# Inverting the softmax sums from doubled rows in DRAM in a four-layer attention kernel

## The chip, the core and the metric

The kernel runs on one core of a Trainium2 chip. The metric is the device time of one execution in microseconds. Before the change it is 1423.88 us, the median of 3 runs (1420.51 to 1424.61).

The core has TensorE (PE in the profile; PEld is its weight load), VectorE (DVE), ScalarE (ACT), GpSimd (POOL) and SyncE (SP), each with an in-order queue of its own. Nearly all transfers are issued from SyncE's queue, a few small ones from ScalarE's; sixteen DMA engines carry them.

## The reference, cut to what matters

Four residual layers run over 2048 tokens of width 512 with 32 heads of 16: A, B, A, B. Layer A is a linear attention with learned feature maps; layer B splits the tokens into four segments of 512 and mixes, per head, causal softmax attention inside the segment with a memory of the earlier segments:

```python
def phi(t): return jnp.where(t > 0, t + 1.0, jnp.exp(t))
for s in range(4):                       # segments of 512 tokens
    qs, ks, vs = q[:, :, s], k[:, :, s], v[:, :, s]
    p = softmax(qs @ ks.T * scale + mask)
    a_dot = p @ vs
    a_mem = (phi(qs) @ M) / ((phi(qs) @ z)[..., None] + 1e-6)
    outs.append(g * a_mem + (1.0 - g) * a_dot)
    M, z = M + phi(ks).T @ vs, z + phi(ks).sum()
x = x + concat(outs) @ wo
```

Both `a_dot` and `a_mem` are a numerator over a sum for each token and head. These divisions are what the change is about.

## The kernel before

**Layout.** In layer B the data of a segment lie transposed: heads and their 16 features along the 128 partitions, the 512 tokens along the row. A chunk `c` (0 to 3) is one such tile and holds eight heads. A turn `m` (32 in a layer) is half a chunk: segment, chunk, half `hf` with four heads. `LayerB.steps` walks through five steps in each turn and places every other piece of work (projections, output products, loads) at a step written by hand; `at(k + j, f)` puts a function on step `k + j`, `due` calls it. The wrappers `Ordered` and `mm` tie every instruction to the one before it on its engine, so each queue runs in the order of the program text.

**A turn on the engines.** SyncE copies projected queries and keys into the operand tiles (`stack`, six transfers a chunk half; `e<-ta` in the profile). TensorE computes logits twice: once for the row maxima (`maxima`; the banks `mx` and `my`, reduced by VectorE), once for the weights (`attend`; bank `lg`, exponentials by ScalarE, the causal triangle cut by GpSimd's affine selects). The maxima are transposed, negated and written by a transfer from ScalarE's queue into a row of the query tile (`put_maxima`; `e<-mt`). TensorE multiplies the weights by the values (`weighted`; bank `pv`), ScalarE moves the result into tile `U`, which holds numerators and sums.

**The division.** A numerator tile has 128 partitions (eight heads of 16 features), but there are only eight rows of sums, one for each head. They go through DRAM:

- `gather` (L1136) writes the half's numerators to the tile `num` (`tmp<-U`) and its four rows of sums to the DRAM tile `den` (`den<-U`).
- For the memory part `read` (L1076) writes four rows of sums from each of two tiles (`den<-mmq`, `den<-ot`).
- `invert` (L1110) has four steps. `compact` loads the sums as a dense tile over 128 partitions: 64 columns wide (`dn`) where both parts are there, 32 (`dm`) where there is one. `flip` is a reciprocal on VectorE. `put` writes it back to DRAM (`inv<-dn`, `inv<-dm`). `load` reads, for each part, eight rows of 512, each repeated sixteen times, into a tile of 128 partitions (`KN<-inv` for the attention's part, `mmq<-inv` for the memory's).
- `close` (L1145) has GpSimd multiply numerators by inverted sums (`tmp<-tmp,KN` and `ot<-ot,mmq`) and add the parts; ScalarE and GpSimd split the sum into a high and a low part for the output product.

The steps come from the tables `GATHER`, `READ`, `INVERT` and `JOIN`; the two loads of one chunk are issued together, and often `stack`'s copies of the next chunk half stand right behind them. The two layers B have 32 inversions (20 with `dn`, 12 with `dm`) and 52 such loads of 256 KB each. In the last segment of a layer only some chunks go this way; the others are divided on VectorE after a transposition (`finish`).

Of the kernel before, what the change touches and what calls it, by code (L numbers as in the profile page):

```python
# [15 lines left out]
D = 512  # L16
H = 32
DH = 16
P = 128
# [106 lines left out]
def interleave_kernel(ctx, tc, x_in, a_wqkv, a_wphi, a_wo, b_wq, b_wk, b_wv, b_wo, b_beta,  # L126
# [15 lines left out]
    def nm(s):  # L142
        uid[0] += 1
        return f"{s}_{uid[0]}"

    def T2(tag, bufs, dt=F32, shape=(P, 512)):
        return sp.tile(list(shape), dt, tag=tag, bufs=bufs, name=nm(tag))

    def PS(tag, bufs, shape=(P, 512)):
        return ps.tile(list(shape), F32, tag=tag, bufs=bufs, name=nm(tag))  # L150
# [38 lines left out]
    dve, act, pool, sync = [Ordered(e) for e in (nc.vector, nc.scalar, nc.gpsimd, nc.sync)]  # L189
# [10 lines left out]
    def mm(*a, **k):  # L200
        n = a[0].free_size()
        work[0] += n / 2.26 if k["rhs"].dtype == F32R else (n * 2 / 2.4 + 25 if "tile_position" in k else 2 * max(112, n * 2 / 2.4))
        return held(nc.tensor.matmul(*a, **k))  # L203
# [55 lines left out]
    def dtile(shape, name):  # L259
        return dr.tile(list(shape), F32, name=name)  # L260
# [745 lines left out]
    class LayerB:  # L1006
# [69 lines left out]
        def read(self, s, c, k):  # L1076


            kn, ph = self.summed(s, c)[1], self.st[s, c]["phi", 0]
            pn = [PS("pv", PV), PS("g", G)]  # L1080
            for a in range(2):
                mm(pn[a][0:68, :], lhsT=kn[64 * a : 64 * a + 64, :], rhs=ph[64 * a : 64 * a + 64, :],
                   start=True, stop=True, tile_position=(64 * a, 0))
            old = self.old[s, c] = T2("ot", OT)
            upper = T2("mmq", 2)
            for t, p in zip((old, upper), pn):
                act.activation(t[0:68, :], p[0:68, :], AF.Identity, bias=bd[0:68, 26:27])

            def dens():
                d = self.den(s, c)  # L1090
                for a, t in enumerate((upper, old)):
                    sync.dma_start(out=d[12 - 4 * a : 16 - 4 * a], in_=t[64:68, :])

            def numerators():
                sync.dma_start(out=old[64:128, :], in_=upper[0:64, :])
            self.at(k + READ[0], dens)
            self.at(k + READ[1], numerators)
            if s == NSEG - 1 and c >= self.cut:
                self.invert(s, c, k + READ[2], range(1, 2), INVERT[2][c])

                def scaled():
                    pool.tensor_tensor(out=old, in0=old, in1=self.inv.pop((s, c, 1)), op=MUL)
                self.at(k + READ[3], scaled)

        def den(self, s, c):
            if (s, c) not in self.dens:
                self.dens[s, c] = dtile((16, D), nm("den"))
            return self.dens[s, c]

        def invert(self, s, c, k, parts, steps):  # L1110


            lo, hi = 8 * parts[0], 8 * parts[-1] + 8
            n = (hi - lo) * 4
            tiles = {}

            def compact():
                d = tiles["d"] = T2("dn" if n == 64 else "dm", 1, shape=(P, n))
                sync.dma_start(out=d[:, 0:n], in_=self.den(s, c)[lo:hi].rearrange("h (x i) -> (h x) i", i=n))

            def flip():
                dve.reciprocal(tiles["d"][:, 0:n], tiles["d"][:, 0:n])

            def put():
                tiles["i"] = dtile((hi - lo, D), nm("inv"))
                sync.dma_start(out=tiles["i"].rearrange("h (x i) -> (h x) i", i=n), in_=tiles["d"][:, 0:n])

            def load():
                for i in parts:
                    t = self.inv[s, c, i] = T2(*(("mmq", 2) if i else ("KN", 1)))  # L1130
                    rows = tiles["i"][8 * i - lo : 8 * i - lo + 8].unsqueeze(1).broadcast_to([8, DH, D])
                    sync.dma_start(out=t, in_=rows)
            for j, f in zip(steps, (compact, flip, put, load)):
                self.at(k + j, f)

        def gather(self, s, c, hf, U):  # L1136
            if hf == 0:
                self.num[s, c] = T2("tmp", 2)
            sync.dma_start(out=self.num[s, c][64 * hf : 64 * hf + 64, :], in_=U[1 - hf : P : 2])
            sync.dma_start(out=self.den(s, c)[4 * hf : 4 * hf + 4], in_=U[31 * hf : P : 32])  # L1140

        def outputs(self, s, c):
            return [T2("oh", OO, F32R), T2("ol", OO, F32R)]
# [518 lines left out]
```

## Time and profile before

| what | value |
|---|---|
| median of 3 runs | 1423.88 us |
| profiled execution | 1420.89 us, span 1419.2 us |
| granted TensorE clock | 0.999 |
| transfers of all DMA queues | 222.72 MB, 157 GB/s in the mean |
| loads of inverted sums | 28 to `KN`, 24 to `mmq` |
| writes of sums | 56 from `U`, 24 from `mmq`, 24 from `ot` |

The span runs from the first to the last instruction of one profiled execution; the 1.7 us beside it lie around it. Lines of a group give busy time, the mean of one instruction in ns, and the idle time of the engine just before with what ended it. Most engine instructions go through one helper and bear its line, L181; matmuls bear L203, transposes L207; so groups are told apart by the names of the tiles, written as result<-operands. In a timeline row the brackets give the engine's idle time ahead of the instruction and what ended it. A stretch of windows has its length, the engines' busy times, the granted clock, the mean share of the sixteen DMA engines and GB/s.

### The profile page before, as it was taken

To read this page: it belongs to the slowest core of one execution; us is meant where nothing else is said; L and a number is where in the kernel's file an instruction comes from. 1 tells how busy PE (TensorE), PEld (TensorE's weight loads), DVE (VectorE), ACT (ScalarE), POOL (GpSimd) and SP (SyncE) were. 2 spreads that over 40 slices of the span, in tenths; PEclk is the share of its full clock that TensorE was granted. 3 is DMA by queue.
4 is the path that set the end of the run, shared out by engine and by line. 5 is a ranking of instruction groups with operands and counts; after the bars stand their busy time and mean duration, and the time that the engine had idled before them with its cause. 6 is when DMAs were issued, how large, how long until landed. Compare 5 with 4: busy or idle time off the path is not lost.

```text
span 1419.2 us, 33171 instructions
## 1 busy us (share of the span) xinstructions
PE 1373.8 (97%) x12070; PEld 946.3 (67%) x12070; DVE 953.1 (67%) x3028; ACT 810.0 (57%) x1246; POOL 733.8 (52%) x1073
## 2 busy tenths in 40 slices
PE   9999999999999999999999999999999999999997
PEld 7787778765666565665568887886656565666554
DVE  5766888677666556577546768958776665666663
ACT  5555345447676576566544434553666765765654
POOL 1678765325566556554524446641446565654543
PEclk9999999999999999999999999999999999999999
DMA  5369285536655546466640104854465565555541
GB/s 196 119 220 335 92 267 187 173 115 186 186 132 167 167 133 179 147 162 196 173 146 31 61 31 132 266 177 144 129 185 147 148 182 158 146 165 145 142 143 68
DMA packets 134898, 222.72 MB, mean 157 GB/s; under 512 B 26032, under 2 KB 39472, under 8 KB 134736
## 3 DMA queue, kind: packets, MB, share of 16 engines
q1 hardware_dynamic: 132768, 219.96, 52.0%
q8 instruction: 97, 1.59, 0.5%
q10 hardware_dynamic: 1968, 0.64, 0.2%
q14 instruction: 65, 0.53, 0.1%
HBM read 115.54 MB, written 41.55 MB: 111 GB/s over the span
## 4 chain that ended last, share of the span: by engine, by line
PE 74%; DVE 7%; ACT 6%; DMA 5%; POOL 4%; issue 2%; SPq 1%; ACTq 0%; DVEq 0%; POOLq 0%
PE g L203 45%; PE pv L203 8%; PE lg L203 8%; PE mx L203 4%; PE g L207 3%; ACT P L181 3%; PE my L203 3%; POOL P L181 2%; PE lg L207 2%; DMA e<-ta 1%; SPq L181 1%; DVE es L181 1%; POOL tb L181 1%; POOL tmp L181 1%; DVE junk L181 1%
## 5 line engine op out<-in xcount | busy, mean ns | idle before, releaser
L181 ACT ACTIVATE P<-lg 128x1024 f32<-128x1024 f32 x316 | 324.8, 1028 | 172.5 <-PE lg L203 152.0
L181 POOL TENSOR_SCALAR_AFFINE_SELECT P<-P 128x256 f32<-128x256 f32 (+1 forms) x448 | 190.1, 439 | 399.0 <-ACT P L181 394.8
L181 DVE CUSTOM_DVE_ANT_0 junk<-mx,mask 128x128 uint8<-128x128 f32 (+2 forms) x384 | 147.2, 421 | 116.3 <-PE my L203 86.8
L203 PE MATMUL g<-hh,wqk 128*128 128x512 f32 x512 | 185.2, 410 | 0.7 <-ACT mt L181 0.7
L203 PE MATMUL lg<-e,e 64*128 64x512 f32 (+1 forms) x1010 | 166.3, 387 | 12.3 <-ACT P L181 10.8
L203 PE MATMUL g<-w,oh 128*128 128x512 f32 x508 | 169.5, 414 | 0.5 <-ACT hh L181 0.4
L203 PE MATMUL pv<-P,v 128*32 128x512 f32 (+3 forms) x2048 | 165.1, 439 | 4.4 <-ACT ot L181 4.3
L181 DVE CUSTOM_DVE_ANT_0 mx<-mx,mask 128x512 f32<-128x512 f32 x128 | 89.1, 696 | 114.6 <-PE my L203 93.6
L203 PEld LDWEIGHTS lg<-e,e 64*128 64x128 f32 x1010 | 80.1, 184 | 109.9 <-issue 50.7
L203 PE MATMUL my<-e,e 63*128 63x256 f32 (+3 forms) x519 | 148.1, 345 | 4.3 <-DVE mxs L181 3.2
L203 PE MATMUL mx<-e,e 63*128 63x256 f32 (+3 forms) x519 | 147.0, 336 | 2.2 <-DVE mxs L181 1.9
L181 DVE CUSTOM_DVE_ANT_0 junk<-my,mask 128x128 uint8<-128x128 f32 (+2 forms) x384 | 146.7, 420 | 0.0
L203 PE MATMUL g<-w,hh 128*128 128x512 f32 x448 | 144.0, 402 | 0.3 <-ACT hh L181 0.3
L203 PEld LDWEIGHTS pv<-P,v 128*32 128x32 f32 x2048 | 53.6, 109 | 106.4 <-issue 93.9
L203 PEld LDWEIGHTS g<-hh,wqk 128*128 128x128 f32 x512 | 96.2, 188 | 32.3 <-issue 11.8
L203 PEld LDWEIGHTS g<-w,oh 128*128 128x128 f32 x508 | 87.9, 189 | 30.3 <-issue 13.2
L203 PE MATMUL g<-w,ol 128*128 128x512 f32 x254 | 101.2, 398 | 2.9 <-DVE ol L181 2.1
L203 PE MATMUL g<-hl,wqk 128*128 128x512 f32 x256 | 100.3, 392 | 0.0
L181 DVE DVE_READ_ACCUMULATOR2_ANT mxs<- 128x1 f32 x1024 | 100.1, 98 | 0.0
L203 PEld LDWEIGHTS mx<-e,e 63*128 63x128 f32 (+1 forms) x519 | 90.5, 186 | 11.1 <-DVE mxs L181 4.8
L203 PEld LDWEIGHTS g<-w,hh 128*128 128x128 f32 x448 | 80.3, 188 | 22.9 <-issue 6.3
L203 PEld LDWEIGHTS my<-e,e 63*128 63x128 f32 (+1 forms) x519 | 83.9, 185 | 16.9 <-DVE mxs L181 8.7
(189 smaller groups left out, 2835.9 us busy)
## 6 DMA issues: line engine op xcount, KB each, us to landing
e<-ta SPq DMA_DIRECT2D x384, 128.0 KB
wqk<-wqk SPq DMA_DIRECT2D x64, 512.0 KB
x<-x SPq DMA_DIRECT2D x48, 256.0 KB
xr<-x SPq DMA_DIRECT2D x32, 256.0 KB
x<-xr SPq DMA_DIRECT2D x28, 256.0 KB
tmp<-U SPq DMA_DIRECT2D x56, 128.0 KB
KN<-inv SPq DMA_DIRECT2D x28, 256.0 KB
pq<-tb SPq DMA_DIRECT2D x24, 256.0 KB
```

Source lines behind the costliest of these rows:

```text
L181: i = f(*a, **k)
L203: return held(nc.tensor.matmul(*a, **k))
L207: return held(nc.tensor.transpose(*a))
```

## The change

Each row of sums is written to DRAM twice, by a transfer whose source repeats the row; the DRAM tile has 16 rows of 2 x 512. `compact` and `put` carry twice as much, so the dense tiles are 128 and 64 columns wide. The DRAM tile of inverted sums then has each row twice in a row, and `load` takes sixteen rows, each repeated eight times. The values that arrive in the 128 partitions are the same. No step of the tables is changed.

```diff
             def dens():
                 d = self.den(s, c)
                 for a, t in enumerate((upper, old)):
-                    sync.dma_start(out=d[12 - 4 * a : 16 - 4 * a], in_=t[64:68, :])
+                    sync.dma_start(out=d[12 - 4 * a : 16 - 4 * a], in_=t[64:68, :].unsqueeze(1).broadcast_to([4, 2, D]))
...
-                self.dens[s, c] = dtile((16, D), nm("den"))
+                self.dens[s, c] = dtile((16, 2, D), nm("den"))
...
             lo, hi = 8 * parts[0], 8 * parts[-1] + 8
-            n = (hi - lo) * 4
+            n = (hi - lo) * 8
...
             def compact():
-                d = tiles["d"] = T2("dn" if n == 64 else "dm", 1, shape=(P, n))
-                sync.dma_start(out=d[:, 0:n], in_=self.den(s, c)[lo:hi].rearrange("h (x i) -> (h x) i", i=n))
+                d = tiles["d"] = T2("dn" if n == P else "dm", 1, shape=(P, n))
+                sync.dma_start(out=d, in_=self.den(s, c)[lo:hi].rearrange("h u (x i) -> (h u x) i", i=n))

             def flip():
-                dve.reciprocal(tiles["d"][:, 0:n], tiles["d"][:, 0:n])
+                dve.reciprocal(tiles["d"], tiles["d"])

             def put():
-                tiles["i"] = dtile((hi - lo, D), nm("inv"))
-                sync.dma_start(out=tiles["i"].rearrange("h (x i) -> (h x) i", i=n), in_=tiles["d"][:, 0:n])
+                tiles["i"] = dtile((2 * (hi - lo), D), nm("inv"))
+                sync.dma_start(out=tiles["i"].rearrange("h (x i) -> (h x) i", i=n), in_=tiles["d"])

             def load():
                 for i in parts:
                     t = self.inv[s, c, i] = T2(*(("mmq", 2) if i else ("KN", 1)))
-                    rows = tiles["i"][8 * i - lo : 8 * i - lo + 8].unsqueeze(1).broadcast_to([8, DH, D])
+                    rows = tiles["i"][2 * (8 * i - lo) :][0:16].unsqueeze(1).broadcast_to([16, DH // 2, D])
                     sync.dma_start(out=t, in_=rows)
...
-            sync.dma_start(out=self.den(s, c)[4 * hf : 4 * hf + 4], in_=U[31 * hf : P : 32])
+            sync.dma_start(out=self.den(s, c)[4 * hf : 4 * hf + 4],
+                           in_=U[31 * hf : P : 32].unsqueeze(1).broadcast_to([4, 2, D]))
```

## The prediction

> **What bounds the kernel now.** I read the page's busy times, then the chain that ended last, then the chain in order of time, then TensorE's own idle times, and last the DMA around the loads that the change touches.
>
> ```profile
> span 1419.2 us, 33171 instructions
> PE 1373.8 (97%) x12070; PEld 946.3 (67%) x12070; DVE 953.1 (67%) x3028; ACT 810.0 (57%) x1246; POOL 733.8 (52%) x1073
> PE 74%; DVE 7%; ACT 6%; DMA 5%; POOL 4%; issue 2%; SPq 1%; ACTq 0%; DVEq 0%; POOLq 0%
> ```
>
> TensorE is busy 1373.8 of 1419.2 us, so about 45 us are all that any unhidden wait can give back. The chain puts 5% on DMA. What the change can win must be found where a late transfer holds TensorE up, and that is a few short places. First, how wide the loads of the inverted sums run (timeline of SyncE's queue, then windows; the last two columns are the mean busy share of the 16 DMA engines and GB/s):
>
> ```profile
> 695.48 0.60 SPq L181 DMA_DIRECT2D mmq<-inv  x1
> 702.60 2.82 SPq L181 DMA_DIRECT2D e<-awk  x6
> ...
> 697.50:698.50 1.00, 1.00 (x12) 0.61 (x5) 0.40 (x2) 0.29 (x1) 0.31 (x1) 1.00 0.50 177
> 703.50:705.50 2.00, 2.00 (x11) 1.35 (x10) 1.93 (x5) 1.02 (x3) 1.54 (x3) 1.00 0.86 223
> ```
>
> From 697.5 to 698.5 almost nothing but two of these loads is under way (`KN<-inv` was issued just ahead of `mmq<-inv`), and the share stands at 0.50; once plain weight loads have joined, at 703.5, it is 0.86. Loads of eight rows repeated sixteen times keep half of the engines busy and leave the other half idle. Their effect on what is queued behind them (chain in order of time: start, us, what):
>
> ```profile
> 529.47 7.05 DMA mmq<-inv
> 586.98 5.97 DMA e<-ta
> 653.10 2.49 DMA e<-ta
> 694.75 5.68 DMA KN<-inv
> 972.78 2.48 DMA ot<-x
> ```
>
> A plain 256 KB load took 2.48 us and a 128 KB copy of projected rows 2.49 us where the queue was free; the row loads, 256 KB too, took 5.68 and 7.05 us, and a copy issued right behind a pair of them 5.97 us.
>
> **The change part by part.** Gains first. TensorE's idle times that I trace back to such a landing (timelines of TensorE, then of ScalarE, VectorE and GpSimd):
>
> ```profile
> 483.27 0.56 PE L203 MATMUL lg<-e,e 64*128 64x256 f32 x4 [0.95 <-ACT P L181]
> 540.01 0.56 PE L203 MATMUL lg<-e,e 64*128 64x256 f32 x4 [0.43 <-ACT P L181]
> 681.18 1.28 PE L203 MATMUL pv<-P,v 128*32 128x512 f32 x16 [1.15 <-ACT ot L181]
> 683.15 0.50 PE L203 MATMUL lg<-e,e 64*128 64x512 f32 x2 [0.69 <-DMA mmq<-inv]
> 687.34 0.46 PE L203 MATMUL mx<-e,e 63*128 63x512 f32 x1 [0.50 <-DVE mxs L181]
> 702.21 0.56 PE L203 MATMUL lg<-e,e 64*128 64x256 f32 x4 [0.71 <-ACT P L181]
> 1179.19 0.56 PE L203 MATMUL lg<-e,e 64*128 64x256 f32 x4 [0.79 <-ACT P L181]
> 1370.80 1.28 PE L203 MATMUL pv<-P,v 128*32 128x512 f32 x16 [0.50 <-ACT ot L181]
> 1373.89 0.38 PE L203 MATMUL mx<-e,e 63*128 63x256 f32 x1 [1.10 <-DVE mxs L181]
> ...
> 538.37 0.52 ACTq L181 DMA_DIRECT2D e<-mt  x1
> 538.93 1.02 ACT L181 ACTIVATE P<-lg 128x1024 f32<-128x1024 f32 x1 [2.56 <-DMA mmq<-inv]
> 701.13 1.02 ACT L181 ACTIVATE P<-lg 128x1024 f32<-128x1024 f32 x1 [1.03 <-DMA KN<-inv]
> 1178.12 1.02 ACT L181 ACTIVATE P<-lg 128x1024 f32<-128x1024 f32 x1 [1.28 <-DMA e<-ta]
> 685.82 0.69 DVE L181 TENSOR_TENSOR xr<-g,xr 128x512 f32<-128x512 f32 x1 [4.35 <-DMA xr<-x]
> 674.59 1.30 POOL L181 TENSOR_TENSOR tmp<-tmp,KN 128x512 f32<-128x512 f32 x1 [6.66 <-DMA mmq<-inv]
> ```
>
> ScalarE's exponentials stand behind an issue of the maxima row (538.37), and that issue waits for an earlier transfer that is none of its data; so a late row load stops ScalarE, and TensorE misses the freed bank of the logits. How much sooner the loads land I take from the clean window: two loads, 512 KB, at half the engines. If the same bytes use all of them, their moving part halves. A lone row load has 2.48 us as its floor (the plain load), so a single one gains at most 5.68 - 2.48 = 3.2 us and a copy behind a pair at most 5.97 - 2.49 = 3.5 us; at the low end 0, since the bytes stay. In crowded stretches all engines are busy already:
>
> ```profile
> 588.00:592.00 4.00, 4.00 (x32) 2.48 (x31) 2.87 (x12) 2.05 (x2) 1.33 (x3) 1.00 0.94 233
> 670.00:675.00 5.00, 5.00 (x41) 3.02 (x40) 3.00 (x12) 2.63 (x3) 0.41 (x1) 1.00 0.76 200
> 1172.00:1176.00 4.00, 4.00 (x32) 2.55 (x24) 2.61 (x12) 1.62 (x2) 1.86 (x3) 1.00 0.99 246
> ```
>
> With a share of 0.94 to 0.99 spreading saves less there than at 0.76. I take 1.2 us sooner in crowded stretches, 2 us in the others.
>
> - 483.27 and 1179.19: ScalarE's wait of 1.28 us loses most of its length; of 0.95 + 0.79 = 1.74 us I take 1.5.
> - 540.01: the wait of 2.56 us shrinks below 1; with the small stops just behind it 0.6.
> - 681 to 703: GpSimd would start its product 2 us sooner (674.59), but selects that wait for exponentials stand between, so 0.7 of the 1.15 us; of 0.69 I take 0.3; the residual load (4.35 us of VectorE's waiting) comes 1 us sooner, 0.5; at 702.21 all 0.7. Sum 2.2.
> - 1370.80 to 1373.89: the first gap only, 0.5. The second is ended by VectorE behind a plain load, whose delay I cannot put on the row load before it.
> - Scattered waits of ScalarE behind copies, as at 586.98: 0.6.
>
> Gains: 1.5 + 0.6 + 2.2 + 0.5 + 0.6 = 5.4 us; bounds 0 and, all the rows listed with 0.6 of scattered ones, 0.95 + 0.43 + 1.15 + 0.69 + 0.50 + 0.71 + 0.79 + 0.50 + 1.10 + 0.6 = 7.4 us.
>
> Costs. The inversion works on twice the columns (groups by line; issues by tile, with least, median and longest ns; VectorE's timeline):
>
> ```profile
> L181 DVE RECIPROCAL dn<-dn 128x64 f32<-128x64 f32 x20 | 11.0, 548 | 0.4 <-DMA dn<-den 0.4
> L181 DVE RECIPROCAL dm<-dm 128x32 f32<-128x32 f32 x12 | 4.2, 348 | 2.2 <-DMA dm<-den 2.2
> ...
> L181 SPq DMA_DIRECT2D den<-U x56: 522/542/607, 324.0 to 1367.7; - x56
> L181 SPq DMA_DIRECT2D den<-mmq x24: 266/436/876, 385.2 to 1374.1; - x24
> L181 SPq DMA_DIRECT2D den<-ot x24: 271/288/623, 386.1 to 1374.5; - x24
> L181 SPq DMA_DIRECT2D KN<-inv x28: 628/657/670, 338.0 to 1384.6; - x28
> L181 SPq DMA_DIRECT2D xr<-x x32: 343/430/1171, 429.6 to 1374.8; - x32
> ...
> 526.65 0.55 DVE L181 RECIPROCAL dn<-dn 128x64 f32<-128x64 f32 x1
> 530.37 0.42 DVE L181 CUSTOM_DVE_ANT_0 junk<-mx,mask 128x256 uint8<-128x256 f32 x1 [1.52 <-PE my L203]
> ```
>
> 32 more columns cost 548 - 348 = 200 ns. So 20 inversions grow by 400 ns and 12 by 200: 8.0 + 2.4 = 10.4 us of VectorE. Behind the one at 526.65 stand four maxima, then VectorE idles 1.52 us for TensorE: 0.4 us fits into that. The idle time is the cover; without it all 10.4 us would show. I take the chain's 7% of VectorE, 0.7 us; bounds 0 and 10.4.
>
> The 104 writes of sums (56 + 24 + 24) carry 16 KB for 8 KB. Repeating rows makes an issue dearer by at most 657 - 430 = 227 ns, by these rows, and by nothing at least: 0 to 24 us of SyncE; I take 100 ns, 10 us. SyncE is 1% of the chain, hence 0.1 us. Behind a write SyncE waits for its landing before it may issue the compacting load, and behind that stand six copies; then it waits for the longer reciprocal before the write back. Only one of these waits is near TensorE, the late `dm` in the table (2.2 us in all): 0.2 us. The compacting loads and the write backs move 64 KB for 32 in runs twice as long, as many runs as before: nothing, covered by the steps between. Costs: 0.7 + 0.1 + 0.2 = 1.0 us.
>
> Net: 5.4 - 1.0 = 4.4 us less. The profiled execution took 1420.9 us (span 1419.2 and 1.7 around it), so 1416.5; it lies 3.0 us under the median of the runs, 1423.9, and against that the sum is 1419.5.
>
> [...]
>
> **The rivals.**
>
> *Hidden anyway.* TensorE sets the pace, other transfers fill the engines (0.94 to 0.99), and the steps of the schedule leave room. Each stop above also has a second cause: at 540 the same place in the second layer, without the wait of 2.56 us, still shows idle time (1243.05 below). Then gain and cost cancel: 1423.9 less 0 to 2, about 1423.
>
> ```profile
> 1243.05 0.49 PE L203 MATMUL lg<-e,e 64*128 64x512 f32 x2 [0.59 <-ACT P L181]
> ```
>
> *Slower through the inversion.* The longer reciprocal sits in VectorE's in-order queue ahead of the maxima whose banks TensorE waits for. It decides if the idle time behind an inversion is under the 0.4 us added. At 526.65 it is not. If 0.4 us shows at the 20 large ones and the gains do not come: 1423.9 + 8 = 1432; with half of the gains, 1429.
>
> *It does not spread.* The number of engines could follow something other than the sixteen rows, or eight engines could be a limit of reading one row many times. Then the costs alone are left: 1423.9 + 1 = 1425. The share of 0.86 with weight loads shows only that other shapes spread.
>
> **How the numbers follow.** Main forecast 0.58, hidden 0.15, slower through the inversion 0.20, no spread 0.07. A measurement of this kernel can tell about 0.3% from no change: 1419.6 and 1428.2 are the limits. Of the main case 0.40 lies under 1419.6 and 0.18 inside, gains of half the size (1423.9 - 2.7 + 1.0 = 1422.2) among them; of the hidden one 0.01 under, 0.12 inside, 0.02 above; the inversion gives 0.03 inside and 0.17 above; no spread 0.04 inside and 0.03 above. So faster 0.41, same 0.37, slower 0.22. The main case alone runs from 1423.9 - 7.4 = 1416.5, less 3 for the spread of the runs, 1413, to 1423. The range goes from there to 1429, the inversion with half of the gains.
>
> **What would show it.** Right: the share while only row loads run near 0.9 or more and not 0.5; chain entries of copies behind them of 3 to 5 us; no wait of 2.56 us at 538.9 and less at 483, 681 and 702; reciprocals of some 950 and 550 ns without a new idle time of TensorE behind them. Wrong: a share of still 0.50; or the share doubled and TensorE's idle time unchanged (hidden); or new waits of TensorE for maxima right behind reciprocals, or for copies behind a SyncE that waits for the sums. A time above 1428 or below 1413 would mean that I have missed a mechanism.

## The result and the profile after

| | before | after |
|---|---|---|
| median | 1421.12 us (16 runs, 1416.73 to 1424.61) | 1417.42 us (16 runs, 1415.16 to 1419.61) |
| ratio to before, 95% interval | | 0.9977 [0.9966, 0.9987] |
| profiled execution | 1420.89 us, span 1419.2 us | 1417.35 us, span 1415.6 us |

The change makes the kernel faster by 0.23%: 3.7 us between the medians, 3.6 us between the two profiled spans. The forecast was 4.4 us. The median of before fell from 1423.88 us to 1421.12 us as more runs came in, so of the two forms of the forecast only the difference is to be compared. The sixteen runs of before spread over 7.9 us, twice the effect: a single stop in a single profiled execution proves little, and the experiments below are read by their ratios first.

The page of the changed kernel, its span, busy times and shares of the chain that ended last:

```profile
span 1415.6 us, 33171 instructions
PE 1371.6 (97%) x12070; PEld 944.6 (67%) x12070; DVE 961.9 (68%) x3028; ACT 810.2 (57%) x1246; POOL 734.0 (52%) x1073
PE 73%; DVE 8%; ACT 6%; POOL 5%; DMA 3%; issue 3%; SPq 1%; ACTq 0%; DVEq 0%; POOLq 0%
```

DMA's share of the chain goes from 5% to 3%, VectorE's from 7% to 8%. That is the direction which the prediction had laid out, but it shows little: e2 and e6 below, with the short reciprocals of before, have VectorE at 9%. TensorE's own busy time falls by 2.2 us though it runs the same 12070 matmuls; that is read at the end of the layer, below. Two stretches of the changed kernel (length, five engines, granted clock, DMA share, GB/s):

```profile
697.50:698.50 1.00, 1.00 (x12) 0.57 (x5) 0.45 (x2) 0.25 (x1) 0.36 (x1) 1.00 0.90 246
670.00:675.00 5.00, 5.00 (x41) 3.17 (x39) 1.99 (x7) 1.59 (x2) 0.19 (x1) 1.00 1.03 273
```

Where the share stood at 0.50 with two row loads alone under way it is 0.90, at 177 and 246 GB/s; the stretch from 670 went from 0.76 to 1.03. The loads do spread over about twice as many engines. The copy behind row loads that ends in the stop at 483 is quicker by a third (chain in order of time, before, then after):

```profile
474.92 6.58 DMA e<-ta
```

```profile
475.94 4.41 DMA e<-ta
...
667.10 7.73 DMA mmq<-inv
```

That is within the 3 to 5 us of the forecast. The row load in the crowd of weight loads is no quicker: 7.73 us, for 5.68 and 7.05 us in the chain of before. TensorE's stops, the same places as in the prediction:

```profile
482.80 0.56 PE L203 MATMUL lg<-e,e 64*128 64x256 f32 x4 [0.16 <-ACT P L181]
539.13 0.56 PE L203 MATMUL lg<-e,e 64*128 64x256 f32 x4
...
622.39 0.57 PE L203 MATMUL lg<-e,e 64*128 64x256 f32 x4 [0.76 <-ACT P L181]
667.58 0.38 PE L203 MATMUL mx<-e,e 63*128 63x256 f32 x1 [1.92 <-DVE mxs L181]
681.78 1.29 PE L203 MATMUL pv<-P,v 128*32 128x512 f32 x16 [0.51 <-ACT ot L181]
683.74 0.49 PE L203 MATMUL lg<-e,e 64*128 64x512 f32 x2 [0.68 <-ACT P L181]
701.87 0.56 PE L203 MATMUL lg<-e,e 64*128 64x256 f32 x4 [0.33 <-ACT P L181]
1178.22 0.56 PE L203 MATMUL lg<-e,e 64*128 64x256 f32 x4 [0.15 <-ACT P L181]
1369.96 1.28 PE L203 MATMUL pv<-P,v 128*32 128x512 f32 x16 [0.52 <-ACT ot L181]
1371.85 0.38 PE L203 MATMUL mx<-e,e 63*128 63x256 f32 x1
```

The start times of the same matmul in the two executions give a running account:

| matmul | before | after | shift so far |
|---|---|---|---|
| `lg`, first layer B | 483.27 | 482.80 | -0.47 |
| `lg` behind the 2.56 us wait | 540.01 | 539.13 | -0.88 |
| `pv` behind the last segment's divisions | 681.18 | 681.78 | +0.60 |
| `lg` | 702.21 | 701.87 | -0.34 |
| `lg`, second layer B | 1179.19 | 1178.22 | -0.97 |
| `pv`, end of the second layer B | 1370.80 | 1369.96 | -0.84 |
| `mx` behind it | 1373.89 | 1371.85 | -2.04 |

About a microsecond is won by 540, lost again between 540 and 681, where two stops are new (622.39 and 667.58), won back by 1178, and the rest of the 3.6 us comes in the last 50 us.

The longest new stop is the one at 667.58. SyncE's queue of the changed kernel ahead of it, then of the kernel before:

```profile
655.39 0.69 SPq L181 DMA_DIRECT2D den<-mmq  x1
656.13 0.68 SPq L181 DMA_DIRECT2D den<-ot  x1
656.86 4.11 SPq L181 DMA_DIRECT2D w<-awv  x4
662.42 0.45 SPq L181 DMA_DIRECT2D dm<-den  x1
```

```profile
656.49 1.91 SPq L181 DMA_DIRECT2D w<-awv  x4
659.79 1.41 SPq L181 DMA_DIRECT2D dm<-den  x1
```

Four issues of weight loads took 4.11 us in place of 1.91, and the compacting load behind them went out 2.6 us later. VectorE then stands still with its reciprocal, and behind it in its order are the maxima that TensorE waits for:

```profile
666.33 0.55 DVE L181 RECIPROCAL dm<-dm 128x64 f32<-128x64 f32 x1 [2.26 <-DMA dm<-den]
```

Of the weight loads' issues between 650 and 664 (least, median and longest ns) only one was held:

```profile
L181 SPq DMA_DIRECT2D w<-awv x5: 422/433/2616, 656.9 to 663.9; - x5
```

This stop is no fixed price of the change: the other kernels that carry its costs, with loads of other rows or distances, have 1.77 us (e1), 0.59 us (e11), 0.45 us (e9) and less than 0.3 us (e10) at this place, and the kernel before has 0.33 us.

The end of the layer has two parts. VectorE adds the residual of a chunk late in the kernel before, and not late in the changed one:

```profile
1372.48 0.69 DVE L181 TENSOR_TENSOR xr<-g,xr 128x512 f32<-128x512 f32 x1 [3.79 <-issue]
```

```profile
1370.43 0.69 DVE L181 TENSOR_TENSOR xr<-g,xr 128x512 f32<-128x512 f32 x1 [2.60 <-PE mx L203]
```

That is the 1.10 us of the second gap. The other part is in the clock (windows of before, then of after; the third number from the end is the granted clock):

```profile
1374.00:1378.00 4.00, 3.73 (x15) 2.40 (x17) 2.41 (x11) 0.27 (x1) 1.76 (x3) 0.72 0.61 186
1378.00:1382.00 4.00, 3.97 (x35) 2.06 (x34) 2.46 (x11) 2.62 (x3) 0.90 (x3) 0.86 0.04 6
```

```profile
1374.00:1378.00 4.00, 4.00 (x38) 2.27 (x37) 3.30 (x10) 2.36 (x3) 1.69 (x3) 1.00 0.57 131
1378.00:1382.00 4.00, 3.12 (x19) 1.86 (x17) 3.91 (x18) 1.75 (x3) 1.40 (x3) 1.00 0.24 78
```

Behind the stop the granted clock of before is 0.72 and 0.86 in these two windows; that is (1 - 0.72) x 4 + (1 - 0.86) x 4 = 1.7 us of TensorE's work. (In windows of 1 us from 1375 to 1380 it is 0.87, 0.50, 0.50, 0.50 and 0.93.) It is the larger part of the 2.2 us by which its busy time differs, and with the 1.1 us of the stop it makes the 2.8 us that the profile shows for the end: the shift goes from -0.84 us at 1370.80 to -3.6 us at the end of the span.

What the change charges, by groups of the changed kernel:

```profile
L181 DVE RECIPROCAL dn<-dn 128x128 f32<-128x128 f32 x20 | 19.0, 948 | 0.0
L181 DVE RECIPROCAL dm<-dm 128x64 f32<-128x64 f32 x12 | 6.6, 548 | 3.5 <-DMA dm<-den 3.5
...
L181 SPq DMA_DIRECT2D den<-U x56: 562/571/802, 323.8 to 1366.7; - x56
L181 SPq DMA_DIRECT2D den<-mmq x24: 681/695/909, 385.7 to 1372.1; - x24
L181 SPq DMA_DIRECT2D den<-ot x24: 631/677/754, 386.5 to 1372.8; - x24
L181 SPq DMA_DIRECT2D inv<-dn x20: 319/382/580, 441.2 to 1375.8; - x20
```

The reciprocals take 948 and 548 ns, as forecast. The issues of the doubled writes grew by 29, 259 and 389 ns (from medians of 542, 436 and 288), together 56 x 29 + 24 x 259 + 24 x 389 ns = 17.2 us of SyncE's time.

### The profile page after: what moved, and what is told of

Its sections match the earlier page's. It is cut to its first block, busy times and chain, and to the rows that moved or that the text cites. A ratio compares the mean times of both kernels' runs of the same rounds, so it can differ in the third digit from the quotient of the medians.

```text
span 1415.6 us, 33171 instructions
## 1 busy us (share of the span) xinstructions
PE 1371.6 (97%) x12070; PEld 944.6 (67%) x12070; DVE 961.9 (68%) x3028; ACT 810.2 (57%) x1246; POOL 734.0 (52%) x1073
## 4 chain that ended last, share of the span: by engine, by line
PE 73%; DVE 8%; ACT 6%; POOL 5%; DMA 3%; issue 3%; SPq 1%; ACTq 0%; DVEq 0%; POOLq 0%
PE g L203 45%; PE pv L203 8%; PE lg L203 8%; PE mx L203 4%; PE g L207 3%; ACT P L181 3%; PE my L203 3%; POOL P L181 2%; PE lg L207 2%; DVE es L181 1%; SPq L181 1%; POOL tb L181 1%; DMA e<-ta 1%; POOL tmp L181 1%; DVE junk L181 1%
## 5 line engine op out<-in xcount | busy, mean ns | idle before, releaser
L203 PE MATMUL lg<-e,e 64*128 64x512 f32 (+1 forms) x1010 | 166.1, 386 | 10.7 <-ACT P L181 10.2
```

## The experiments

Each kernel was timed against the kernel before on the same chip; a ratio of 1.001 is 1.4 us. "Rows apart" is the distance in DRAM between the rows that one load repeats. The kernel before and the changed one have 2 KB.

| kernel | rows x repeats, rows apart | ratio, 95% interval | median us | span us |
|---|---|---|---|---|
| the change | 16 x 8, 2 KB | 0.9977 [0.9966, 0.9987] | 1417.42 | 1415.6 |
| e1_wide_rows8 | 8 x 16, 4 KB | 1.0074 [1.0058, 1.0089] | 1431.59 | 1430.3 |
| e2_put_twice | 16 x 8, 2 KB | 1.0008 [0.9998, 1.0018] | 1421.3 | 1417.9 |
| e4_rows4 | 4 x 32, 4 KB | 1.0432 [1.0415, 1.045] | 1479.59 | 1474.2 |
| e5_later_flip | 16 x 8, 2 KB | 0.998 [0.9971, 0.9988] | 1417.34 | 1416.0 |
| e6_sums_twice | 8 x 16, 2 KB | 0.9996 [0.9983, 1.0008] | 1420.55 | 1419.3 |
| e7_wide_flip | 8 x 16, 2 KB | 1.0014 [1.0001, 1.0027] | 1422.43 | 1420.3 |
| e8_put_twice_rows8 | 8 x 16, 4 KB | 1.0103 [1.0084, 1.0123] | 1436.19 | 1431.7 |
| e9_wide_adjacent | 8 x 16, 2 KB | 1.0021 [1.0009, 1.0032] | 1424.81 | 1425.1 |
| e10_rows16_4k | 16 x 8, 4 KB | 1.001 [1.0001, 1.0019] | 1422.54 | 1423.0 |
| e11_rows16_pad | 16 x 8, 2304 B | 0.9998 [0.999, 1.0007] | 1420.99 | 1416.8 |
| e12_rows8_4k | 8 x 16, 4 KB | 1.005 [1.0038, 1.0062] | 1426.74 | 1424.0 |
| e13_rows8_pad | 8 x 16, 2304 B | 1.0029 [1.0018, 1.0039] | 1425.39 | 1424.0 |

**The whole change without the wider loads.** From the changed kernel, the loads take every second row, which are the eight distinct ones:

```diff
-rows = tiles["i"][2 * (8 * i - lo) :][0:16].unsqueeze(1).broadcast_to([16, DH // 2, D])
+rows = tiles["i"][2 * (8 * i - lo) :][0:16:2].unsqueeze(1).broadcast_to([8, DH, D])
```

> Everything of the change but its last step: sums written twice, compacted, inverted and stored at double width, and then the loads read eight rows repeated sixteen times, as before. Theory (the gain comes from the loads' use of all DMA engines): only the costs are left, ratio to the kernel before 1.001, some 1 us slower, and the wait of ScalarE near 538.9 us and TensorE's idle 0.9 us near 483 are there again. Rival (the gain comes from something else in the change, such as the longer runs of the compacted sums): the ratio stays near the change's, 0.997.

It measured 1.0074, far over both. The stop at 483 is there again (2.15 us), that at 540 is not. The rows read are those of before, as many of them, repeated as often; but they lie 4 KB apart and not 2, which the expectation did not count. So the run says nothing yet about the loads' width, and the distance had to be taken out by itself (e9 to e13).

**The wider loads without the wider reciprocals.** From the kernel before, the write-back goes out twice into a doubled tile:

```diff
-tiles["i"] = dtile((hi - lo, D), nm("inv"))
-sync.dma_start(out=tiles["i"].rearrange("h (x i) -> (h x) i", i=n), in_=tiles["d"][:, 0:n])
+tiles["i"] = dtile((hi - lo, 2, D), nm("inv"))
+for u in range(2):
+    sync.dma_start(out=tiles["i"][:, u].rearrange("h (x i) -> h x i", i=n), in_=tiles["d"][:, 0:n])
...
-rows = tiles["i"][8 * i - lo : 8 * i - lo + 8].unsqueeze(1).broadcast_to([8, DH, D])
+rows = tiles["i"].rearrange("h u n -> (h u) n")[2 * (8 * i - lo) :][0:16].unsqueeze(1).broadcast_to([16, DH // 2, D])
```

> Sums, compaction and reciprocal of the kernel before; only the write back of the inverted sums is issued twice, into the two halves of a doubled DRAM tile, and the loads read sixteen rows repeated eight times. Theory (gain from the loads, costs from the wider reciprocal and the dearer writes of sums): the gain of the change without these costs, less 32 more issues of 0.35 us on SyncE, which stand before the loads: ratio 0.9965, as much as the change or up to 1 us better. Rival (the costs of the change are hidden anyway, so there is nothing to save, and the second write delays the loads): 0.998 or above.

It measured 1.0008, in the rival's range: no gain is left. The issues of the write-backs in this kernel:

```profile
L181 SPq DMA_DIRECT2D inv<-dn x40: 539/589/1012, 440.1 to 1378.1; - x40
...
L181 SPq DMA_DIRECT2D inv<-dm x24: 597/624/637, 336.2 to 1385.3; - x24
```

There are 64 of them for 32, with medians of 589 and 624 ns where the changed kernel issues `inv<-dn` in 382. Their number and their dearer form were not measured apart. How the rows are doubled decides whether doubling pays.

**A quarter of the engines.** From the kernel before, loads of four rows, each repeated 32 times:

```diff
-rows = tiles["i"][8 * i - lo : 8 * i - lo + 8].unsqueeze(1).broadcast_to([8, DH, D])
+rows = tiles["i"][8 * i - lo : 8 * i - lo + 8][0:8:2].unsqueeze(1).broadcast_to([4, 2 * DH, D])
```

> The kernel before, with loads that read four rows (every second one) repeated thirty-two times in place of eight repeated sixteen times: the same bytes and issues, and half of the heads get another head's inverted sum. Theory (a load runs on as many engines as its rows allow): a quarter of the engines, DMA share near 0.25 while only these loads run, landings of 8 to 10 us, and TensorE waits for them: ratio 1.004 to 1.010, 6 to 14 us slower. Rival (transfers are hidden, TensorE sets the pace): within 0.999 to 1.002.

The direction is right, the size is four to ten times that: 1.0432, some 61 us. The page of this kernel, two windows in which almost nothing but row loads is under way, and two entries of its chain of waits (start, us):

```profile
span 1474.2 us, 33171 instructions
PE 1388.6 (94%) x12070; PEld 955.8 (65%) x12070; DVE 952.2 (65%) x3028; ACT 810.4 (55%) x1246; POOL 734.8 (50%) x1073
PE 62%; DMA 14%; DVE 10%; ACT 6%; issue 3%; SPq 3%; POOL 2%; ACTq 1%; DVEq 0%; POOLq 0%
```

```profile
728.00:729.00 1.00, 1.00 (x14) 0.51 (x16) 0.00 (x0) 0.27 (x1) 0.38 (x2) 1.00 0.27 92
729.00:730.00 1.00, 0.88 (x16) 0.20 (x8) 0.00 (x0) 0.68 (x1) 0.97 (x1) 1.00 0.25 92
```

```profile
445.04 8.95 DMA e<-ta
...
538.25 11.34 DMA mmq<-inv
```

The DMA share is the expected quarter, 0.25 to 0.27, after 0.50 with eight rows and 0.90 with sixteen. A row load of 7.05 us now takes 11.34, a copy behind row loads 8.95 us, and DMA is 14% of the chain. Part of it comes through the clock again:

```profile
670.00:675.00 5.00, 4.19 (x18) 3.02 (x20) 1.47 (x8) 2.36 (x3) 3.98 (x6) 0.66 0.37 111
```

The granted clock is 0.66 in this stretch, and TensorE's busy time for the same matmuls is 1388.6 us, 14.8 more than before, of the 55.0 us by which the span is longer. The price of fewer engines is thus steep: half of them cost some 6 us against all (e9 below), a quarter another 61 against half. The four rows also lie 4 KB apart; but eight rows at that distance cost only 0.5% (e12), so most of this is the number of rows. (Half of the heads of this kernel are divided by another head's sum; its instructions are as many and its transfers as large as before.)

**Reciprocals out of TensorE's way.** From the changed kernel, the reciprocals of the memory sums of chunks 2 and 3 in the last segment come one step later:

```diff
-(2.5, 4.5, 5.5, 7.5)
+(2.5, 5.5, 5.5, 7.5)
```

> The changed kernel, with the reciprocals of the memory's sums of chunks 2 and 3 in the last segment of each layer one step later (5.5 for 4.5). Theory (the changed kernel's one new stop, VectorE's wait of 2.26 us for the compacted sums at 666 us with 1.92 us of TensorE's idle time behind it, comes from the later landing): that stop goes, ratio to the kernel before 0.9965, 1 to 1.5 us better than the change. Rival (a stop there comes from the crowd of weight loads, and TensorE then waits for the copies behind them): the same ratio as the change, 0.9975.

It measured 0.998 [0.9971, 0.9988], the same as the change. The stop at 667 is gone from this kernel, but TensorE waits for a weight load a little later, and 1.67 us ahead of `pv`, where the changed kernel waits 0.51:

```profile
668.29 0.50 PE L203 MATMUL g<-w,hh 128*128 128x512 f32 x1 [0.52 <-DMA w<-awv]
679.66 1.28 PE L203 MATMUL pv<-P,v 128*32 128x512 f32 x16 [1.67 <-ACT ot L181]
```

So the stop of 1.92 us was not worth 1.92 us: other stops took its place. This is no faster version.

**The writes of sums alone, the wider reciprocals alone.** Both from the kernel before:

```diff
-sync.dma_start(out=d[12 - 4 * a : 16 - 4 * a], in_=t[64:68, :])
+sync.dma_start(out=d[:, 12 - 4 * a : 16 - 4 * a].rearrange("u h n -> h u n"), in_=t[64:68, :].unsqueeze(1).broadcast_to([4, 2, D]))
...
```

```diff
-dve.reciprocal(tiles["d"][:, 0:n], tiles["d"][:, 0:n])
+e = tiles["e"] = T2("dn2" if n == 64 else "dm2", 1, shape=(P, 2, n))
+dve.reciprocal(e, tiles["d"][:, 0:n].unsqueeze(1).broadcast_to([P, 2, n]))
...
```

> The kernel before, with one part of the change alone: every row of sums is written to DRAM twice (into two copies of the sums' tile); compaction, reciprocal, write back and loads are those of before and read the first copy. Theory A (the 10 us that the change costs without its wider loads come from SyncE's in-order queue: dearer issues of the writes, 0.69 for 0.29 to 0.44 us, and later landings for which SyncE waits with six copies behind): most of it is here, ratio 1.004 to 1.006. Theory B (they come from VectorE's longer reciprocals): 1.000 to 1.001.

> The kernel before, with the reciprocal alone at double width: it reads the same columns twice and writes 2 x 64 or 2 x 32 columns, of which the first half is written back. It adds 0.4 us to 20 reciprocals and 0.2 us to 12, 10.4 us of VectorE. Theory A (SyncE's queue makes the cost): 1.000 to 1.001. Theory B (the reciprocals do): 1.004 to 1.007.

The doubled writes of e6 cost nothing that can be measured (0.9996). But they are not the writes of the change. Their two copies go to two separate halves of the tile, and in this form two of the three issues are not dearer:

```profile
L181 SPq DMA_DIRECT2D den<-mmq x24: 272/444/774, 386.4 to 1374.3; - x24
L181 SPq DMA_DIRECT2D den<-ot x24: 270/289/728, 386.9 to 1374.6; - x24
```

Medians of 444 and 289 ns are those of before (436 and 288); the change has 695 and 677. So e6 prices the doubled bytes, and no run prices the dearer issues, 15.6 of the 17.2 us above, by themselves. The wider reciprocals cost 0.14%, 2.0 us with an interval from 0.1 to 3.8: more than the 0.7 us of the prediction, less than the theory by which each of them shows.

**Two write-backs with eight rows.** The kernel of e2, with loads of the eight distinct rows, which in its doubled tile lie 4 KB apart:

```diff
-rows = tiles["i"].rearrange("h u n -> (h u) n")[2 * (8 * i - lo) :][0:16].unsqueeze(1).broadcast_to([16, DH // 2, D])
+rows = tiles["i"][8 * i - lo : 8 * i - lo + 8, 0].unsqueeze(1).broadcast_to([8, DH, D])
```

> The kernel with the write back issued twice, but with loads of eight rows repeated sixteen times (every second row of the doubled tile). Against that kernel (1.0008) it shows the wider loads alone. Theory (the wider loads give some 14 us, as the change at 0.9977 against its own form with eight rows at 1.0074): 1.009 to 1.011, 10 us or more of cost by the second write. Rival (wider loads give the predicted 5.4 us, and the form with eight rows was slow for another reason): 1.003 to 1.006.

1.0103 lies in the expected band, but the agreement counts for little, since width and distance change together in the step from e2.

**The whole change without the wider loads, at the old distance.** As e1, but with eight adjacent rows, 2 KB apart:

```diff
-rows = tiles["i"][2 * (8 * i - lo) :][0:16].unsqueeze(1).broadcast_to([16, DH // 2, D])
+rows = tiles["i"][8 * i - lo :][0:8].unsqueeze(1).broadcast_to([8, DH, D])
```

> As the change with loads of eight rows repeated sixteen times, but the eight rows lie next to each other in DRAM (the two copies of four heads' rows, so half of the heads get another head's inverted sum), where the first form read every second row. Theory (the number of rows, not their distance, made that one slow): the same ratio, 1.006 to 1.009. Rival (rows 4 KB apart are read more slowly): 1.000 to 1.002, what the costs of 1 us would give.

1.0021 [1.0009, 1.0032]: against e1 only the choice of rows differs, and it is worth 0.53%. (Fewer heads than the expectation says get their own sum, and where both parts are inverted together the memory's load reads rows of the attention's part. The number of instructions and the bytes moved are the same as in e1.) This is the control that the change needed. All of its costs are in it and none of the wider loads: 0.21% or 3.0 us (1.3 to 4.5). From it to the change, 0.9977 / 1.0021 = 0.9956, some 6.3 us are the gain of the sixteen rows; with intervals of 0.1% on both sides that is good to about 2 us. TensorE's stops in this kernel:

```profile
454.90 0.56 PE L203 MATMUL lg<-e,e 64*128 64x256 f32 x4 [1.25 <-ACT P L181]
485.36 0.57 PE L203 MATMUL lg<-e,e 64*128 64x256 f32 x4 [1.02 <-ACT P L181]
683.08 1.28 PE L203 MATMUL pv<-P,v 128*32 128x512 f32 x16 [0.50 <-ACT ot L181]
1379.76 0.38 PE L203 MATMUL mx<-e,e 63*128 63x256 f32 x1 [1.37 <-DVE mxs L181]
```

All the logits' waits of a kernel are in one row of the groups (busy, mean ns, then idle before): of e9, then of the changed kernel, then of before.

```profile
L203 PE MATMUL lg<-e,e 64*128 64x512 f32 (+1 forms) x1010 | 166.1, 386 | 14.1 <-ACT P L181 13.5
```

```profile
L203 PE MATMUL lg<-e,e 64*128 64x512 f32 (+1 forms) x1010 | 166.1, 386 | 10.7 <-ACT P L181 10.2
```

```profile
L203 PE MATMUL lg<-e,e 64*128 64x512 f32 (+1 forms) x1010 | 166.3, 387 | 12.3 <-ACT P L181 10.8 <-DMA mmq<-inv 0.7
```

The wider loads take 3.4 us of these waits away (14.1 to 10.7); the stops at 454.90 and 485.36 are most of it. The stop of `pv` is 0.50 us here with eight rows as it is 0.51 in the changed kernel with sixteen, and it is 1.67 us in e5 and 1.02 us in e10, with sixteen too: its fall from 1.15 us cannot be put on the width.

**The distance by itself.** Each width at 4 KB and at 2304 B. From the changed kernel (e10, e11) and from the kernel before (e12, e13):

```diff
-tiles["i"] = dtile((2 * (hi - lo), D), nm("inv"))
+tiles["i"] = dtile((2 * (hi - lo), 2 * D), nm("inv"))[:, 0:D]   # e11: D + 64 in place of 2 * D
...
-tiles["i"] = dtile((hi - lo, D), nm("inv"))
+tiles["i"] = dtile((hi - lo, 2 * D), nm("inv"))[:, 0:D]         # e13: D + 64
...
```

> The changed kernel with the rows of the inverted sums 4 KB apart in DRAM in place of 2 KB; loads still take sixteen rows repeated eight times. Theory A (the engines a load runs on decide, the distance matters only with half of them): 0.997 to 0.999, as the change. Theory B (the distance of the rows decides, and the change gains because it reads more distinct rows close together): 1.002 or above, some 7 us worse than the change, as between the two forms with eight rows.

> The changed kernel with the rows 2304 bytes apart (64 columns unused between them). Theory A: as the change, 0.997 to 0.999. Theory B (an even distance makes repeated reads meet at one place of the memory): better than the change, 0.994 to 0.996.

> The kernel before with nothing but the rows of the inverted sums 4 KB apart in DRAM in place of 2 KB. If the distance made the first form with eight rows slower than the second (1.0074 against 1.0021), it costs the same here: 1.004 to 1.007, with later landings of the loads. If it did not (that difference came from the two forms' different rows), 0.999 to 1.001.

> The kernel before with the rows 2304 bytes apart. Theory A (half of the engines is the limit of these loads): 0.999 to 1.001. Theory B (the place in memory is): 0.996 to 0.998, the change's gain without its engines.

| rows apart | 8 x 16 | 16 x 8, with the change's costs |
|---|---|---|
| 2 KB | 1 (before) | 0.9977 |
| 2304 B | 1.0029 | 0.9998 |
| 4 KB | 1.0050 | 1.0010 |

Sixteen rows are quicker than eight at each distance, by 0.23, 0.31 and 0.40%, and that with the change's costs on their side. And each width has its highest ratio at 4 KB. The logits' row of e12 shows the waits grow:

```profile
L203 PE MATMUL lg<-e,e 64*128 64x512 f32 (+1 forms) x1010 | 166.5, 387 | 15.5 <-ACT P L181 14.8
```

A tile with gaps between its rows is also written back in another form, whose issues are dearer (medians of 546 and 622 ns in e12, 548 and 624 in e13, for 343 and 421 before), so a comparison with 2 KB does not isolate the reads. Between 2304 B and 4 KB the form is the same, and 4 KB costs 0.21% with eight rows; the 0.12% with sixteen is at the edge of the intervals. The pair e1 and e9 isolates the reads at 4 and 2 KB: the same writes, and other rows read.

## Why the prediction was right, and where it was off

- **Bound and mechanism: right.** Late row loads hold up a few places of TensorE; sixteen rows spread over about twice the engines. The shares of 0.25, 0.50 and 0.90 with four, eight and sixteen rows and e4's 1.0432 show it from both sides, so the rival by which nothing spreads falls; e9 against the change disposes of the one by which the transfer is hidden anyway. Rows times repeats are 128 in every form, so no run tells whether the engines follow the number of rows or the number of repeats. That sixteen rows would use all sixteen engines was the author's assumption from the 0.50 with eight; no trace of before has a row load of sixteen rows. The gains of half the size, 2.7 us, that stand among the forecast's chances rest on no trace, and no run shows them; the runs show about 6.3.
- **Gains, 5.4 us: about 6.3, good to some 2 us, and only in part at the places listed.** At 483 and 1179 the term holds: the forecast was 1.5 us of 1.74, and the stops went from 1.74 to 0.31. In all five profiled kernels with sixteen rows both stops are 0.15 to 0.17 us; in the eight with eight rows 13 of the 16 are 0.57 to 2.15 us and the other three 0.16 or 0.17. At 540 the stop went; but no other profiled kernel has it, of either width, so the 0.6 us is not shown to be the loads'. From 681 to 703 the prediction had 2.2 us. GpSimd's product did not start 2 us sooner there (674.81 for 674.59); the fall of `pv` by 0.64 us is not the width's; the stop behind `mmq<-inv` stayed (0.69 and 0.68 us), that at 702 fell by 0.38. What the loads save there stands against the stop of 1.92 us just ahead. The place at 454 was on no list: six of the eight kernels with eight rows stop there for 0.52 to 2.04 us, and of the five with sixteen only e2, for 0.30.
- **The end of the layer: the wrong gap.** The prediction credited 0.5 us to the first gap at 1370.80, which stayed (0.52), and nothing to the second, which went (1.10) and with it the dip of the clock. Whether the loads did that is not settled: with sixteen rows the changed kernel, e5 and e11 have no stop over 0.41 us there, but e2 and e10 have 1.89 and 1.25; with eight rows seven kernels have 1.10 to 2.61 and e7 has none.
- **Costs, 1.0 us: 3.0 (1.3 to 4.5).** This is the step that was mis-sized. The reciprocals were put at 0.7 us by their share of the chain; alone they cost 2.0 (0.1 to 3.8, e7). The writes of sums were put at 0.1 us. Their doubled bytes cost nothing measurable (e6), but the bound of 227 ns for a dearer issue was wrong (`den<-ot` grew by 389 ns), and what the dearer issues cost is not shown. The late `dm` was put at 0.2 us and made a stop of 1.92 in this one execution, behind an issue of SyncE that the prediction did not look at; e5 shows that removing it wins nothing by itself, and e9, with the same costs, has 0.45. Doubled bytes and reciprocals alone make 0.10% against the 0.21% of e9; the rest is within the intervals and stays open, with the dearer issues as the untested candidate.
- **The rival of the slower inversion: wrong in size.** Its 8 us would need every reciprocal to show its 0.4 us. A fifth of the 10.4 us showed.
- **The rival by which transfers are hidden: one reading was wrong.** It takes the stop at 1243.05 for the second layer's counterpart of the one at 540.01. By the order of the logits it is the counterpart of one at 547.66, also 0.59 us; that of 540.01 starts at 1235.48 and has no stop.
- **The net.** 6.3 and 3.0 us are two parts of one ratio, so their difference of 3.3 us is the change's 0.23% over again and adds nothing to it. Of the forecast's two terms the cost is contradicted, the gain of 5.4 us is not. In the profiled pair 2.8 of the 3.6 us come from a place that was given 0.5 us, so that 4.4 us came so close to 3.7 is in part luck.

## What to carry to other kernels

When a transfer repeats rows to fill partitions, count the rows: the window in which it is alone shows whether it uses all DMA engines (here a share of 0.25, 0.50 and 0.90 with four, eight and sixteen rows), and doubling the rows at their source can pay for itself where every route to the second copy is cheap; a second write-back ate the whole gain here (e2, 1.0008). A control that carries the costs but not the benefit must leave the addresses alone too, or it measures another thing, as e1 did; and a part of a change that is taken alone must keep its form, or the cost stays behind, as in e6. And where single stops come and go between executions by as much as the effect, decide by the control's ratio, and use the stops only to say where.

## What the runs showed of the hardware that was not expected

- **The distance of repeated rows in DRAM matters.** Eight rows each read sixteen times, 4 KB apart in place of 2 KB, cost 0.53% (e9 to e1, the same writes). With the other form of write-back in it, 4 KB costs 0.50% (e12) and 2304 B 0.29% (e13); sixteen rows at 4 KB cost 0.33% against 2 KB (0.9977 to 1.0010). Why adjacent rows are read quicker was not found.
- **A short stop can cost more than its length, and the extra came in one size.** The place at the end of the second layer B in thirteen profiled executions, with the work that TensorE lost to the clock in the following 10 us (one minus the granted clock, summed over windows of 1 us):

  | TensorE's stop there, us | work lost to the clock |
  |---|---|
  | before 1.10, e13 1.12, e10 1.25, e9 1.37, e6 1.38, e12 1.62, e8 2.61 | 1.70 or 1.71 us in each |
  | e1 1.76, e2 1.89 | none |
  | the change none, e7 none, e5 0.26, e11 0.41 | none |

  The lowest granted clock in these windows is 0.50. In before it is 0.50 from 1375.8 to 1379.1 us, and 0.69 and 0.75 in the 0.1 us on either side, which makes the 1.7 us. The length of the stop does not decide: 1.10 us has the dip, 1.89 us has none. What does decide is not shown by any run here.
- **One issue on SyncE's queue can be held for 2.62 us** among others of 0.43 (the weight loads above), with no wait that the profile names. What stood behind it in the queue went out late with it, here the compacting load of the sums, 2.6 us later than in before (662.42 for 659.79). At this place the longest weight issue is 0.55 to 0.71 us in before, e6, e12 and e13, and 1.08 to 2.62 us in the profiled kernels with longer reciprocals or a second write-back; why was not found.
- **The form of a write sets the length of its issue.** Four rows of sums, each written twice, took 677 ns to issue where the two copies lie next to each other (`den<-ot` of the change) and 289 ns where they go to two halves of the tile (e6), the same as 288 ns for one copy.
